# Six experts whose two batches share 448 token slots, routing scratch in PSUM, and weight loads issued at other steps

## The chip, the core and the metric

The kernel runs on one core of one Trainium2 chip. Five engines work at once, each in its own order: TensorE (PE; its weight loads are shown as PEld), VectorE (DVE), ScalarE (ACT), GpSimd (POOL) and SyncE (SP), which here only issues transfers. They wait for each other through semaphores. The metric is device time in microseconds (us) from start to end; lower is better. Of the kernel before, three runs took 550.86, 552.16 and 553.15 us, median 552.16 us.

## The reference

Three layers follow each other. The first is a gated recurrent attention (2 batches, 8 heads, 768 tokens, head size 40), which the kernel computes in chunks of 128 tokens. The second sends each of the 1536 tokens (320 wide) to its two best of 8 experts. The third is one dense layer pair with `h * cos(h)` between them.

```python
noisy_logits = x @ w_gate + np.log1p(np.exp(x @ w_noise)) * noise
top2 = np.argpartition(-noisy_logits, 2, axis=1)[:, :2]
for e in range(E):                       # 8 experts, w1[e]: 320 x 1024, w2[e]: 1024 x 320
    for k in range(2):
        mask = top2[:, k] == e
        h = np.maximum(x[mask] @ w1[e], 0.0)
        out[mask] += top2_w[mask, k, None] * (h @ w2[e])
...
h = x @ w_in                             # 1536 x 2048
g = h * np.cos(h)
return (g @ w_out).astype(np.float32)
```

## The kernel before

**Slots.** A token's row is copied into a slot of its expert, and the expert works on slots. Each expert has, for each batch, 240 slots in two tiles of 120. Experts 0 and 1 run first for batch 0 alone (groups 0 and 1, 240 slots), then experts 2 to 7 for both batches together (groups 2 to 7, four tiles, 480 slots), then experts 0 and 1 for batch 1 (groups 8 and 9). If an expert got more tokens than slots, a branch at the end would compute everything anew; the profile shows nothing of it.

**One expert step.** Each group has eight steps, one for each 128 of the 1024 hidden columns; steps are numbered 0 to 79, and `step(k)` is `expert_step(k // 8, k % 8)`. To keep float32 accuracy, every factor is split into a high part and a low part, each in a format that TensorE takes at full rate. In a step, `split` makes the high part `wh` of the weights two steps ahead on ACT and the low part `wl` on POOL (on DVE for some steps); `mm1` multiplies in eight matmuls, which stream all slots of the group; ACT takes the positive part as `hh`, DVE makes the rest `hl`; and `mm2` of the step before adds, for each tile, `hh x wh`, `hh x wl` and `hl x wh` (320 columns streamed, the tile's slots as the stationary side) into one PSUM bank per tile. After the eighth step `fin1` copies the tiles out (ACT and DVE in turn) and writes them to `YD` in DRAM.

**Routing.** For each batch, `router_a0` to `router_a3` find the two best experts and their weights, `router_b` counts with matmuls at which place of its expert a token stands, `router_b1` and `router_b2` build one-hot matrices, and `router_c` turns them with twelve matmuls into `idx`, the token of each slot. `gather` (an indirect transfer issued by POOL) then fetches the rows into `xgt`, and `prep_slot` transposes them on PE and splits them into `xh` and `xl`. Batch 0 is routed while batch 1 is still in attention; batch 1 after it, during expert steps 5 to 11. Group 2, at step 16, is the first that needs both.

**What sets the order.** Nothing is scheduled by a tool: the code's order is the order on each engine. Attention runs in twelve steps `att_step(n)`; `pre`, `mid`, `fill` and `put` hang other work at places within or behind a step `n`, and `put(k, ...)` behind expert step `k` after attention. Each engine takes its instructions strictly in this order, so an instruction that waits holds all behind it. SP's transfers are one such queue: expert weights (`load_w`, 704 KB for two of eight blocks, into one of two buffers `WB`), results to `YD`, and the third layer's weights (`conv_load`), which DVE and ACT convert during the expert steps (`conv_ops`).

**PSUM.** There are eight banks: four of tag A (`psA`), three of tag S (`psS`), and one of tag M (`psM`). What takes the one M bank (transposes, router matmuls) waits until its last user has been read out.

Of the kernel before, what the change touches and what calls it, by code (L numbers as in the profile page):

```python
# [37 lines left out]
def tile_mlstm_moe_moe2(ctx, tc, qk, kv, og, gi, gf, wcat, noise, wm1, wm2, cst, out):  # L38
# [105 lines left out]
    XD = [dr.tile([S, KW], FT, name=f"xd{b}") for b in range(B)]  # L144
# [272 lines left out]
    def router_b(b):  # L417
        r = R[b]
        p = psM()
        T.matmul(p[:, 0:NC * E + E], tri, os_.rearrange("p c e -> p (c e)"), start=True, stop=False)  # L420
# [9 lines left out]
        ge = rsm([128, 2, NC], "r_ge")  # L430
        V.tensor_scalar(ge, rr, float(SL), None, op0=OP.is_ge)
        pp = rsm([128, 2, NC], "r_pp")
        V.scalar_tensor_tensor(out=pp, in0=ge, scalar=-float(SL), in1=rr, op0=OP.mult, op1=OP.add)
        jj = rsm([128, 2, NC], "r_jj")
        V.scalar_tensor_tensor(out=jj, in0=r["ixf"], scalar=2.0, in1=ge, op0=OP.mult, op1=OP.add)
# [12 lines left out]

    def router_b2(b):
        r = R[b]  # L450
        jj = r["jj"]
# [4 lines left out]
        V.tensor_scalar(bm[:, :, :, 0, :], jm, pid, None, op0=OP.mult)
        V.tensor_tensor(out=bm[:, :, :, 1, :], in0=jm, in1=tid[:, None].to_broadcast([128, 2, NC, 16]), op=OP.mult)

    def router_c(b):
# [8 lines left out]
        hi = rsm([128, 16], "r_hi")
        V.tensor_scalar(hi[:SL], p[:SL, 16:32], 128.0, None, op0=OP.mult)
        idx = r["idx"] = cp.tile([128, 16], U32, name=f"idx{b}")  # L470
        V.tensor_tensor(out=idx[:SL], in0=p[:SL, 0:16], in1=hi[:SL], op=OP.add)


    YD = [dr.tile([NJ * SL, DM], FT, name=f"yd{b}") for b in range(B)]
# [7 lines left out]
    NSL = 4 * SL  # L482
    groups = []
    for e in (0, 1):
        groups.append((e, [(0, 2 * e), (0, 2 * e + 1)]))
    for e in range(2, E):
        groups.append((e, [(0, 2 * e), (0, 2 * e + 1), (1, 2 * e), (1, 2 * e + 1)]))
    for e in (0, 1):
# [587 lines left out]
```

## Time and profile before

| what | us |
|---|---|
| runs, median of three | 552.16 |
| the profiled execution: its own time | 549.69 |
| its span, first to last instruction | 547.1 |
| attention until expert step 5, about | 0 to 113 |
| expert steps 5 to 15 | 113.3 to 148.0 |
| expert steps 16 to 63 (groups 2 to 7) | 148.0 to 322.4 |
| expert steps 64 to 79, first combination | 322.4 to 360 |
| third layer | 360 to 547 |

All stretches are counted from the span's start. An engine that is busy all through a stretch without a gap sets that stretch's length; where it has gaps, the row says what ended each of them. TensorE's clock has two levels; the granted clock of a stretch is its mean share of the full one.

### The profile page before, as it was taken

The page shows a single profiled execution, that of the slowest core. Times are in us where ns is not written, and L with a number is a line of the kernel's source. Part 1 is how long each engine was busy: PE and PEld are TensorE (multiplying, and loading weights), DVE is VectorE, ACT ScalarE, POOL GpSimd, SP SyncE. Part 2 cuts the span into 40 slices and gives each one's busy share as a digit, 9 for nine tenths or more (in the row PEclk, how much of TensorE's full clock was granted, in tenths as well). Part 3 has the DMA queues.
Part 4 walks back from the last instruction along what each step waited for, and adds up shares of the span by engine and source line. Part 5 has one row for each costly group of instructions (what it writes and reads, how often), then busy time and mean ns, then how long its engine had stood idle before and what let it go on. Part 6 is the DMA issues. An engine that isn't in the chain of part 4 may idle for free.

```text
span 547.1 us, 9061 instructions
## 1 busy us (share of the span) xinstructions
PE 506.9 (93%) x3244; PEld 480.0 (88%) x3244; DVE 381.8 (70%) x733; ACT 326.3 (60%) x689; POOL 277.9 (51%) x247
## 2 busy tenths in 40 slices
PE   3899879987699999999999998899999999999994
PEld 2788768987599999999999997799999999999994
DVE  8874585578338687767677458969967756777772
ACT  3567863454345554445445455657878878777772
POOL 6435556647374756576666568746535633300000
PEclk9999998898899999999999999999999999999999
DMA  6888980366383755647283719341101101001001
GB/s 177 245 278 277 315 298 29 97 226 240 101 281 113 234 183 186 232 146 270 92 326 103 287 33 359 118 124 37 37 1 62 48 1 37 2 1 37 0 1 43
DMA packets 25668, 77.67 MB, mean 142 GB/s; under 512 B 3888, under 2 KB 11152, under 8 KB 25616
## 3 DMA queue, kind: packets, MB, share of 16 engines
q1 hardware_dynamic: 22416, 67.18, 36.0%
q0 software_dynamic: 3200, 9.84, 6.2%
q8 instruction: 27, 0.44, 0.3%
q14 instruction: 25, 0.20, 0.1%
HBM read 67.72 MB, written 9.29 MB: 141 GB/s over the span
## 4 chain that ended last, share of the span: by engine, by line
PE 71%; DMA 11%; DVE 8%; POOL 3%; ACT 3%; issue 3%; SPq 0%; POOLq 0%; ACTq 0%; DVEq 0%
PE pS L543 33%; PE pA L552 11%; PE pA L549 11%; PE pA L548 10%; DMA xgt<-xd,idx 4%; DMA qk<-qk 3%; PE pM L505 2%; POOL wl L536 2%; DMA gb<-gd 2%; PE pS L307 1%; ACT wt L206 1%; DMA gd<-g_all 1%; PE pA L244 1%; PE pM L348 1%; DMA raw<-wm 1%
## 5 line engine op out<-in xcount | busy, mean ns | idle before, releaser
L536 POOL TENSOR_TENSOR wl<-wraw,wh 128x704 fp32r<-128x704 f32 x70 | 122.6, 1756 | 84.0 <-ACT wh L534 79.6
L582 DVE SCALAR_TENSOR_TENSOR hl<-pS,hh 128x480 fp32r<-128x480 f32 (+1 forms) x80 | 44.3, 555 | 55.6 <-ACT hh L581 54.9
L534 ACT ACTIVATE wh<-wraw 128x704 fp32r<-128x704 f32 x80 | 63.0, 787 | 23.6 <-PE pA L552 19.8
L549 PE MATMUL pA<-wl,hh 128*120 128x320 f32 x256 | 77.0, 312 | 0.0
L548 PE MATMUL pA<-wh,hh 128*120 128x320 f32 x256 | 76.9, 311 | 0.0
L695 POOL TENSOR_TENSOR hl<-m_t,hh 128x384 fp32r<-128x384 f32 x41 | 41.8, 1020 | 61.4 <-ACT hh L693 40.6
L543 PE MATMUL pS<-xh,wh 128*128 128x480 f32 (+1 forms) x240 | 72.4, 356 | 0.0
L543 PE MATMUL pS<-xh,wl 128*128 128x480 f32 (+1 forms) x240 | 69.1, 342 | 0.3 <-POOL wl L536 0.3
L543 PE MATMUL pS<-xh,w 128*128 128x384 f32 x288 | 66.8, 341 | 0.8 <-DVE m_t L689 0.8
L581 ACT ACTIVATE hh<-pS 128x480 fp32r<-128x480 f32 (+1 forms) x80 | 39.0, 488 | 30.7 <-PE pS L543 30.2
L552 PE MATMUL pA<-wh,hl 128*120 128x320 f32 x256 | 51.7, 314 | 6.0 <-DVE hl L582 6.0
L675 ACT ACTIVATE m_t<-pS,magic 128x384 f32<-128x384 f32 x64 | 37.2, 581 | 28.7 <-PE pS L543 27.6
L543 PEld LDWEIGHTS pS<-xh,w 128*128 128x128 f32 x288 | 49.7, 188 | 1.9 <-DVE m_t L689 1.9
L549 PEld LDWEIGHTS pA<-wl,hh 128*120 128x120 f32 x256 | 47.0, 184 | 1.8
L548 PEld LDWEIGHTS pA<-wh,hh 128*120 128x120 f32 x256 | 47.1, 184 | 1.4
L543 PEld LDWEIGHTS pS<-xh,wl 128*128 128x128 f32 x240 | 43.8, 193 | 4.9 <-POOL wl L536 0.5
L552 PEld LDWEIGHTS pA<-wh,hl 128*120 128x120 f32 x256 | 40.4, 183 | 7.8 <-DVE hl L582 7.8
L507 ACT ACTIVATE xh<-pM 128x360 fp32r<-128x360 f32 (+1 forms) x42 | 20.0, 477 | 45.1 <-PE pM L505 44.9
L689 DVE SCALAR_TENSOR_TENSOR m_t<-m_t,pS 128x384 f32<-128x384 f32 x64 | 35.3, 552 | 12.4 <-ACT m_t L688 12.2
L549 PE MATMUL pA<-w,hh 128*128 128x320 f32 x144 | 42.9, 309 | 0.0
L548 PE MATMUL pA<-w,hh 128*128 128x320 f32 x144 | 42.9, 308 | 0.0
L543 PEld LDWEIGHTS pS<-xh,wh 128*128 128x128 f32 x240 | 41.4, 193 | 1.5
(160 smaller groups left out, 1195.3 us busy)
## 6 DMA issues: line engine op xcount, KB each, us to landing
wraw<-wm SPq DMA_DIRECT2D x36, 704.0 KB
raw<-wm SPq DMA_DIRECT2D x16, 704.0 KB
qk<-qk SPq DMA_DIRECT2D x24, 240.0 KB
gb<-gd SPq DMA_DIRECT2D x10, 512.0 KB
yd<-yt SPq DMA_DIRECT2D x26, 150.0 KB
kv<-kv SPq DMA_DIRECT2D x12, 324.0 KB
wraw<-wm SPq DMA_DIRECT2D x8, 352.0 KB
xd<-xt SPq DMA_DIRECT2D x12, 192.0 KB
```

What stands on the lines that cost most here:

```text
L507: A.activation(xh[:, :, sl], pv, AF.Copy)
L534: A.activation(wh, raw[:, f, :], AF.Copy)
L536: eng.tensor_tensor(out=wl, in0=raw[:, f, :], in1=wh.bitcast(FT), op=OP.subtract)
L543: T.matmul(p[:, :n], w[:, 128 * k:128 * k + 128], x[:, m, :], start=(i == 0), stop=(i == 7))
L548: T.matmul(a[:np_, :DM], hh[:, s], wh[:, KW:], start=first, stop=False)
L549: T.matmul(a[:np_, :DM], hh[:, s], wl[:, KW:], start=False, stop=False)
L552: T.matmul(a[:np_, :DM], hl[:, s], wh[:, KW:], start=False, stop=last)
L581: A.activation(hh[:, :n], p[:, :n], AF.Relu)
L582: V.scalar_tensor_tensor(out=hl[:, :n], in0=p[:, :n], scalar=0.0, in1=hh[:, :n].bitcast(FT), op0=OP.max, op1=OP.subtract)
L675: A.activation(t, m["p"], AF.Identity, bias=magic, scale=0.5 / PI)
L689: V.scalar_tensor_tensor(out=s, in0=s, scalar=1.0, in1=m["p"], op0=OP.subtract, op1=OP.mult)
L695: eng.tensor_tensor(out=m["hl"], in0=m["t"], in1=m["hh"].bitcast(FT), op=OP.subtract)
```

## The change

- Groups 2 to 7 have 448 slots for the tokens of both batches together, in tiles of 128, 128, 128 and 64. The batch 1 ranks of experts 2 to 7 start from batch 0's counts (`router_s`, one more matmul in `router_b`). Groups 0, 1, 8 and 9 keep 240, in tiles of 128 and 112.
- `hh` and `hl` lie in one tile `hb` of 896 columns, so that the 64 `hh` columns and the 64 `hl` columns of the fourth tile are neighbours. `mm2h` loads them as one stationary side of 128 columns and multiplies by `wh` and `wl`: two matmuls where there were three. DVE makes `hl` in two instructions (384 and 64 columns), and `fin1` adds the two halves.
- Much of the router's scratch lies in the M bank (`r["q"]`). For batch 1, `pp`, `jj` and `jm` do too; for batch 0 `r_jj`, `r_pp` and `r_jm` stay in SBUF. One-hot matrices are 128 and 32 wide (before 120 and 16).
- Batch 1's routing calls stand earlier, `prep_slot(1, ...)` uses `psA`, and the low part of step 7's weights is made on POOL.
- Expert 1's weights load behind attention steps 9 to 11 and step 5, expert 2's behind steps 6 to 8 (before 9 to 15). Three transfers behind attention step 8 fill the unused rows of `YD`, which is now one tensor, as is `XD`.

```diff
+    def mm2h(a, wh, wl, hb, first, last):
+        T.matmul(a[:, :DM], hb[:, 384:512], wh[:, KW:], start=first, stop=False)
+        T.matmul(a[:, :DM], hb[:, 384:512], wl[:, KW:], start=False, stop=last)
...
-        V.scalar_tensor_tensor(out=hl[:, :n], in0=p[:, :n], scalar=0.0, in1=hh[:, :n].bitcast(FT),
-                               op0=OP.max, op1=OP.subtract)
+        for a, z, o in ((0, min(n, 384), 512), (384, n, 448)):
+            if a < n:
+                V.scalar_tensor_tensor(out=hb[:, o:o + z - a], in0=p[:, a:z], scalar=0.0,
+                                       in1=hh[:, a:z].bitcast(FT), op0=OP.max, op1=OP.subtract)
...
+            if i == 3:
+                A.activation(t[:64, :DM], a[64:128, :DM], AF.Copy)
+                V.tensor_tensor(out=t[:64, :DM], in0=a[:64, :DM], in1=t[:64, :DM], op=OP.add)
...
-    POOL_SPLIT = (1, 9, 11, 65, 67, 75)
+    POOL_SPLIT = (1, 7, 9, 11, 65, 67, 75)
...
-    for i in range(3):
-        put((6, 7, 6)[i], load_w, 1, 2 + 2 * i, 2)
-    put(5, router_a0, 1)
-    put(5, router_a1, 1)
-    put(5, prep_slot, 1, 0)
-    put(6, prep_slot, 1, 1)
+    put(5, load_w, 1, 6, 2)
     put(5, router_a2, 1)
-    put(7, router_a3, 1)
-    put(7, router_b, 1)
-    put(8, router_b1, 1, 0)
-    put(9, router_b1, 1, 1)
-    put(9, router_b2, 1)
-    put(11, router_c, 1)
+    put(5, prep_slot, 1, 0, psA)
+    put(6, prep_slot, 1, 1, psA)
+    put(6, router_b, 1)
+    put(7, router_b1, 1, 0)
+    put(7, router_b1, 1, 1)
+    put(8, router_b2, 1)
+    put(9, router_p, 1)
+    put(9, router_c, 1)
+    put(10, router_a3, 1)
     for i in range(4):
-        put(11 + i // 2, gather, 2, i)
-        put(13 + i // 2, prep_slot, 2, i)
+        put(10 + i // 2, gather, 2, i)
+        put(12 + i // 2, prep_slot, 2, i)
...
-            put(9 + 8 * i + 2 * h, load_w, e, 2 * h, 2)
+            put(9 + 8 * i + 2 * h if i else (6, 6, 7, 8)[h], load_w, e, 2 * h, 2)
```

`router_a0(1)` and `router_a1(1)` are called before step 5, right behind attention's last matmuls.

**The second matmul pair on PE.** These are PE's rows for the `mm2` of one step of groups 2 to 7 (`pA` is the tile's bank), before:

```order
L548 MATMUL pA<-wh,hh 120x320 [waits Activation_49]
L549 MATMUL pA<-wl,hh 120x320
...
L552 MATMUL pA<-wh,hl 120x320 [waits DVE_49]
L552 MATMUL pA<-wh,hl 120x320 x3
L543 MATMUL pS<-xh,wh 128x480 [waits Activation_49]
```

and now:

```order
L587 MATMUL pA<-wh,hb 128x320 [waits Activation_49]
L588 MATMUL pA<-wl,hb 128x320
...
L591 MATMUL pA<-wh,hb 128x320 [waits DVE_49]
L591 MATMUL pA<-wh,hb 128x320 x2
L599 MATMUL pA<-wh,hb 128x320 [waits DVE_49]
L600 MATMUL pA<-wl,hb 128x320
L582 MATMUL pS<-xh,wh 128x448 [waits Activation_49]
```

The `hh` pair stood four times and stands three times; the fourth tile's pair comes last, behind the three `hl` matmuls.

**Batch 1's routing on DVE**, from the count to the one-hot matrices, before (`hl` and `yt` belong to the expert steps):

```order
L425 TENSOR_TENSOR r_rk<-pM,r_oh_1358 128x96 [waits PE_49]
L427 TENSOR_REDUCE flag<-pM 128x1
L429 TENSOR_REDUCE r_rr<-r_rk 128x12 [waits DVE_49]
L431 TENSOR_SCALAR r_ge<-r_rr 128x12 [waits DVE_49]
L433 SCALAR_TENSOR_TENSOR r_pp<-r_ge,r_rr 128x12 [waits DVE_49]
L435 SCALAR_TENSOR_TENSOR r_jj<-r_ixf,r_ge 128x12
L436 TENSOR_SCALAR r_rr<-r_rr 128x12 [waits DVE_49]
L438 SCALAR_TENSOR_TENSOR r_pos_1443<-r_ixf,r_rr 128x12 [waits DVE_49]
L582 SCALAR_TENSOR_TENSOR hl<-pS,hh 128x240 [waits Activation_49]
L560 COPY yt<-pA 120x320 [waits PE_49]
L446 TENSOR_TENSOR r_am<-cc,r_pp 128x720
```

and now:

```order
L440 TENSOR_TENSOR pM<-pM,r_oh_1356 128x96 [waits DVE_49,PE_49]
L443 TENSOR_REDUCE pM<-pM 128x12 [waits DVE_49]
L444 TENSOR_SCALAR pM<-pM 128x12 [waits DVE_49]
L448 TENSOR_SCALAR r_jj<-pM 128x12 [waits DVE_49]
L449 SCALAR_TENSOR_TENSOR pM<-r_jj,pM 128x12 [waits DVE_49]
L451 TENSOR_SCALAR pM<-pM 128x12 [waits DVE_49]
L637 SCALAR_TENSOR_TENSOR hb<-pS,hb 128x240 [waits Activation_49]
L476 TENSOR_TENSOR r_am<-pM,cc 128x768 [waits DVE_49]
```

The place of a token (`L438`) and the overflow flag are now made later, and every row up to `r_am` has at least one side in the M bank.

**Weight loads on SP** around the end of attention, before:

```order
L480 DMA wraw<-wm 128x1408 [waits DMAHW3_49]
L563 DMA yd_111<-yt 120x320 [waits DMAHW4_49,Activation_49]
L563 DMA yd_111<-yt 120x320 [waits DMAHW5_49,DVE_49]
L480 DMA wraw<-wm 128x1408 [waits DMAHW6_49,Pool_49]
```

and now:

```order
L521 DMA wraw<-wm 128x1408 [waits DMAHW6_49]
L521 DMA wraw<-wm 128x1408 [waits DMAHW0_49,DMAHW7_49,DVE_49,Pool_49]
L521 DMA wraw<-wm 128x1408
L521 DMA wraw<-wm 128x1408 [waits DMAHW1_49]
L616 DMA yd<-yt 128x320 [waits DMAHW2_49,Activation_49]
```

The first load of expert 2 (the row that waits for POOL) stood behind the two writes of group 0's results and stands ahead of them, with two more loads.

## Rows read from the trace of the kernel before

**Rows 1.** The page's first part: busy time of TensorE, share of the span, instructions, and the same of its weight loads and the other engines.

```profile
PE 506.9 (93%) x3244; PEld 480.0 (88%) x3244; DVE 381.8 (70%) x733; ACT 326.3 (60%) x689; POOL 277.9 (51%) x247
```

**Rows 2.** Busy time by stretch: from and to, length, then busy us and instructions of PE, PEld, DVE, ACT and POOL, the granted clock, the share of the DMA engines and GB/s.

```profile
73.80:88.00 14.20, 11.86 (x70) 10.71 (x69) 13.69 (x29) 6.93 (x17) 9.99 (x12) 0.76 0.52 173
...
113.30:148.00 34.70, 26.32 (x194) 24.88 (x193) 22.96 (x70) 15.61 (x34) 17.86 (x13) 0.90 0.59 211
148.00:322.40 174.40, 174.40 (x1023) 162.35 (x1022) 120.74 (x152) 84.90 (x142) 111.20 (x71) 1.00 0.56 193
322.40:360.00 37.60, 33.00 (x247) 30.94 (x247) 30.30 (x48) 21.92 (x43) 31.17 (x23) 1.00 0.55 194
```

**Rows 3.** PE in order of time, from the end of step 22's `mm1` to the start of step 24: start, us from the first's start to the last's end, what, and how many.

```profile
170.71 0.38 PE L543 MATMUL pS<-xh,wl 128*128 128x480 f32 x1
...
172.69 0.47 PE L505 MATMUL pM<-ident,xgt 120*128 120x120 f32 x3
172.92 0.68 PE L543 MATMUL pS<-xh,wh 128*128 128x480 f32 x2
...
174.52 0.38 PE L543 MATMUL pS<-xh,wl 128*128 128x480 f32 x1
174.74 0.31 PE L548 MATMUL pA<-wh,hh 128*120 128x320 f32 x1
...
175.91 0.75 PE L552 MATMUL pA<-wh,hl 128*120 128x320 f32 x4
176.49 0.60 PE L543 MATMUL pS<-xh,wh 128*128 128x480 f32 x2
```

**Rows 4.** The same in the third layer, where a stationary side has 128 columns.

```profile
410.05 0.31 PE L548 MATMUL pA<-w2q,hh 128*128 128x320 f32 x1
410.20 0.31 PE L549 MATMUL pA<-w2q,hh 128*128 128x320 f32 x1
...
410.93 0.60 PE L552 MATMUL pA<-w2q,hl 128*128 128x320 f32 x3
411.37 0.86 PE L543 MATMUL pS<-xh,w 128*128 128x384 f32 x4
```

**Rows 5.** Groups of instructions by line and shape: count, busy us, mean ns of one, idle time before them and what ended it.

```profile
L549 PEld LDWEIGHTS pA<-wl,hh 128*120 128x120 f32 x256 | 47.0, 184 | 1.8
...
L677 DVE SCALAR_TENSOR_TENSOR m_t<-pS,m_t 128x384 f32<-128x384 f32 x64 | 35.7, 558 | 2.2
...
L582 DVE SCALAR_TENSOR_TENSOR hl<-pS,hh 128x480 fp32r<-128x480 f32 x48 | 31.5, 657 | 45.1 <-ACT hh L581 44.6
...
L549 PEld LDWEIGHTS pA<-w,hh 128*128 128x128 f32 x144 | 27.0, 188 | 0.0
...
L582 DVE SCALAR_TENSOR_TENSOR hl<-pS,hh 128x240 fp32r<-128x240 f32 x32 | 12.8, 403 | 10.6 <-ACT hh L581 10.3
```

**Rows 6.** DVE in order of time, during batch 0's routing, batch 1's routing and step 22.

```profile
75.89 1.66 DVE L435 SCALAR_TENSOR_TENSOR r_jj<-r_ixf,r_ge 128x12 f32<-128x12 f32 x1
...
77.66 1.12 DVE L438 SCALAR_TENSOR_TENSOR r_pos<-r_ixf,r_rr 128x12 uint32<-128x12 f32 x1
...
123.23 1.37 DVE L431 TENSOR_SCALAR r_ge<-r_rr 128x12 f32<-128x12 f32 x1
124.63 1.59 DVE L433 SCALAR_TENSOR_TENSOR r_pp<-r_ge,r_rr 128x12 f32<-128x12 f32 x1
126.14 0.16 DVE L435 SCALAR_TENSOR_TENSOR r_jj<-r_ixf,r_ge 128x12 f32<-128x12 f32 x1
...
127.26 0.90 DVE L446 TENSOR_TENSOR r_am<-cc,r_pp 128x720 bf16<-128x720 f32 x1
...
131.10 0.32 DVE L456 TENSOR_SCALAR r_bm<-r_jm,cc 128x192 bf16<-128x192 f32 x1
...
173.84 0.66 DVE L582 SCALAR_TENSOR_TENSOR hl<-pS,hh 128x480 fp32r<-128x480 f32 x1
```

**Rows 7.** POOL in order of time, at the same two routings.

```profile
75.84 1.68 POOL L536 TENSOR_TENSOR wl<-wraw,wh 128x704 fp32r<-128x704 f32 x1 [0.76 <-ACT wh L534]
...
122.87 3.32 POOL L536 TENSOR_TENSOR wl<-wraw,wh 128x704 fp32r<-128x704 f32 x2 [1.03 <-ACT wh L534]
...
131.03 1.00 POOL L497 DMA_INDIRECT xgt<-xd,idx  x1 [0.18 <-issue]
```

**Rows 8.** PE in order of time: batch 1's twelve index matmuls, and its gaps (in brackets the idle time before the row and what ended it).

```profile
81.05 1.22 PE L244 MATMUL pA<-qk 128*128 128x256 f32 x2 [2.20 <-DVE ppt L253]
...
127.00 0.55 PE L552 MATMUL pA<-wh,hl 128*120 128x320 f32 x2 [2.81 <-DVE hl L582]
...
132.52 0.78 PE L465 MATMUL pM<-r_bm,r_am 128*120 128x32 bf16 x12
...
140.74 0.50 PE L505 MATMUL pM<-ident,xgt 120*128 120x120 f32 x3 [2.76 <-DMA xgt<-xd,idx]
...
145.92 0.50 PE L505 MATMUL pM<-ident,xgt 120*128 120x120 f32 x3 [1.35 <-ACT xh L507]
```

**Rows 9.** The chain that ended last, two pieces: start, us, what.

```profile
94.07 3.13 DMA xgt<-xd,idx
...
132.34 8.27 DMA xgt<-xd,idx
```

**Rows 10.** SP's transfers in order of time.

```profile
127.81 1.92 SPq L480 DMA_DIRECT2D wraw<-wm  x4
```

More of the change, by code (lines that the diff above doesn't have):

```diff
@@ L26 @@
 F2 = 2048
-SL = 120
-CAP = 2 * SL
-NJ = 2 * E
+CAP1 = 240
+CAP2 = 448
+NJ = 32
+ROWS = NJ * C
+ROW0 = [0, 256] + [512 * e - 512 for e in range(2, E)]
+ROW1 = [3584, 3840] + ROW0[2:]
 KW = 384
@@ L143, in tile_mlstm_moe_moe2 @@
         STS.append(t)
-    XD = [dr.tile([S, KW], FT, name=f"xd{b}") for b in range(B)]
+    XD = dr.tile([B * S, KW], FT, name="xd")
     KO = H * D
@@ L428, in router_b @@
-        rr = rsm([128, 2, NC], "r_rr")
+        rr, y = (q[:, 440 + 12 * i:452 + 12 * i].rearrange("p (k c) -> p k c", c=NC) for i in range(2))
         V.tensor_reduce(rr, rk, axis=AX.X, op=OP.add)
[L430 to L435, printed above, removed]
@@ L436, in router_b @@
-        V.tensor_scalar(rr, rr, float(CAP - 1), None, op0=OP.min)
-        pos = r["pos"] = rsm([128, 2, NC], f"r_pos{b}", U32)
-        V.scalar_tensor_tensor(out=pos, in0=r["ixf"], scalar=float(CAP), in1=rr, op0=OP.mult, op1=OP.add)
-        r["pp"], r["jj"] = pp, jj
+        V.tensor_scalar(y, rr, -63.75, MAGIC7, op0=OP.add, op1=OP.add)
+        js = rsm([128, 2, NC], "r_jj")
+        jj, pp = ((q[:, 464 + 12 * i:476 + 12 * i].rearrange("p (k c) -> p k c", c=NC) for i in range(2)) if b else
+                  (js, rsm([128, 2, NC], "r_pp")))
@@ L441, in router_b1, with router_s @@
+    def router_s():
+        so = rsm([128, E], "r_so")
+        V.tensor_reduce(so, os_[:, 0:NC].rearrange("p c e -> p e c"), axis=AX.X, op=OP.add)
+        V.tensor_tensor(out=so, in0=so, in1=joint, op=OP.mult)
+        V.tensor_tensor(out=rb[:, 1], in0=so, in1=row1, op=OP.add)
     def router_b1(b, k):
@@ L464, in router_c @@
             for c in range(NC):
-                T.matmul(p[:SL, 0:32], r["am"][:, k, c, :], r["bm"][:, k, c].rearrange("p a j -> p (a j)"),
+                T.matmul(p[:, 0:2 * NJ], r["am"][:, k, c, :], r["bm"][:, k, c].rearrange("p a j -> p (a j)"),
                          start=(n == 0), stop=(n == 2 * NC - 1))
                 n += 1
[L468 to L474, printed above, removed]
+        hi = rsm([128, NJ], "r_hi")
+        if b == 0:
+            V.tensor_scalar(hi, p[:, NJ:2 * NJ], 128.0, None, op0=OP.mult)
+            V.tensor_tensor(out=idx0, in0=p[:, 0:NJ], in1=hi, op=OP.add)
+            V.tensor_scalar(idxe, idx0[:, 0:4], float(S - 1), None, op0=OP.min)
+        else:
+            V.scalar_tensor_tensor(out=hi, in0=p[:, NJ:2 * NJ], scalar=128.0, in1=idx0, op0=OP.mult, op1=OP.add)
+            V.tensor_tensor(out=hi, in0=p[:, 0:NJ], in1=hi, op=OP.add)
+            V.tensor_scalar(idx, hi, float(B * S - 1), None, op0=OP.min)
+    idx0 = cp.tile([128, NJ], FT, name="idx0")
+    idxe = cp.tile([128, 4], U32, name="idxe")
+    idx = cp.tile([128, NJ], U32, name="idx")
+    YD = dr.tile([ROWS, DM], FT, name="yd")
     WB = {}
@@ L480, in load_w @@
         Y.dma_start(WB[e][:, i:i + n, :], wm1[e, :, i:i + n, :])
[L482 to L488, printed above, removed]
-        groups.append((e, [(1, 2 * e), (1, 2 * e + 1)]))
+    T2, T4 = (128, 112), (128, 128, 128, 64)
+    groups = [(e, T2, 2 * e) for e in (0, 1)]
+    groups += [(e, T4, 4 * e - 4) for e in range(2, E)]
+    groups += [(e, T2, 28 + 2 * e) for e in (0, 1)]
     NG = len(groups)
@@ L853, in tile_mlstm_moe_moe2 @@
     mid[9] = [(router_b1, (0, 1))]
+    put(8, router_s)
     fill[9] = [(router_c, (0,)), (gather, (0, 0)), (gather, (0, 1))]
```

197 lines of the change are left out of this document (121 added, 76 removed).

## The prediction

> **What bounds the kernel now.** I read the shares first, then the stretches, then PE's own order, then the gaps and what ended them. PE is busy 506.9 of 547.1 us [rows 1], so only PE's work or PE's gaps can move the time. By stretch the two are apart [rows 2]: in steps 16 to 63 PE is busy 174.40 of 174.40 us at full clock, so that stretch is as long as its matmuls. In steps 5 to 15 it is busy 26.3 of 34.7 us at a mean clock of 0.90, so 8.4 us are gaps, and up to 3.4 us (a tenth of the stretch) go to the lower level, 1.2 instead of 2.4 GHz. The gaps have names [rows 8]: 2.81 us for `hl` from DVE, 2.76 us for gathered rows, 1.35 us for the one M bank between two transposes. DVE was late because `L431` and `L433`, with everything in SBUF and only 12 columns, took 1.37 and 1.59 us where their neighbour took 0.16 [rows 6]; they ended as POOL's two splits did, 3.32 us from 122.87 on [rows 7]. `hl`, which reads PSUM, kept its 403 ns there [rows 5]. The gathered rows were late because four weight transfers had been issued in one burst at 127.81 [rows 10], just ahead of the gather at 131.03 [rows 7]: the next one took 8.27 us to land, where one at 94.07 took 3.13 [rows 9].
>
> **Groups 2 to 7.** Start to start, a matmul of 480 columns takes 0.22 us (174.52 to 174.74) and one of 320 takes 0.147 (1.17 us for eight from 174.74 to 175.91) [rows 3]. That is 0.46 ns a column. 32 columns less on eight matmuls are 8 x 0.0146 = 0.117 us a step, and one matmul of 320 less is 0.147 us. 0.264 us x 48 steps = 12.7 us.
>
> Stationary sides grow from 120 to 128 columns. The third layer has 128, and its matmuls also follow at 0.15 and, over three, 0.44 us [rows 4], so I cost this at nothing: the load (188 ns, before 184 [rows 5]) lies beside the matmul before it. The transposes move nearly as many columns as before, 0.23 us a tile [rows 3]: nothing.
>
> What hides DVE's and ACT's part is the distance from the end of `mm1` to the first `hl` matmul. In step 22 that is 171.09 (170.71 + 0.38) to 175.91 [rows 3], and `hl` ended at 174.50 [rows 6]: 1.41 us to spare. Now the distance loses 0.147 + 0.117 + two `hh` matmuls 0.293 = 0.56 us. `hl` in two instructions costs 558 ns for 384 columns [rows 5], and about 216 ns for 64 by the line through 403 (240 columns) and 657 (480 columns) [rows 5]: 774, so 0.12 us more. About 0.7 us is left. DVE's load rises from 120.7 of 174.4 us [rows 2] to 126.3 of 161.7, 78%. I take no loss, with an upper bound of 4 us: a stall of 0.7 us in about six steps with two weight conversions. The third copy of `fin1` on ACT, and the addition that follows on DVE, come ahead of nine matmuls and an `mm1`, some 2.9 us, before the fourth bank is written again: nothing.
>
> **Steps 5 to 15.** I lay the new order out from 113.3 with the durations of the rows. PE's own work is 26.3 us busy less 3.4 for the clock = 22.9 us; by pieces it is 11 steps x (8 x 0.11 + 6 x 0.147) = 19.4, six transposes of 0.23, and router matmuls of about 1.0 with the twelve that took 0.78 [rows 3, 8], 21.8. I take 22.9. The gaps that I expect:
> - Batch 1's top-two work begins one step earlier on ACT and DVE, and PE reaches the count matmuls at about 117.2; four small DVE rows of 0.2 us end at 117.9. Gap 0.7.
> - The six rows behind the count have a PSUM side, so I cost them at 0.2 us each, not at the 1.4 and 1.6 of rows 6. Then come two `r_am` of 0.95 (0.90 for 720 columns [rows 6], now 768), one `hl`, one copy and three one-hot rows of 0.5 (0.32 for 192 columns [rows 6], now 384): 125.4. PE reaches the twelve matmuls at 123.9. Gap 1.5.
> - `idx` stands at 126.9. POOL's queue has seven splits in a row now (step 7's is new), 1.66 us each [rows 7], and is free at 126.6. Gathers go out at 127.0 and each 1.3 us later, and land 3.1 us later [rows 9]: 130.1 to 134.0. Expert 2's first three transfers left at about 117, when POOL had done step 7's split, so the burst is over. PE asks for the first at 131.6: no gap.
> - Twice, two tiles are prepared back to back through the M bank: 1.3 us each time [rows 8], 2.6.
> - About 0.6 us for `hl` rows that stand behind router rows.
>
> Sum 5.4; the stretch takes 22.9 + 5.4 = 28.3 us, and no gap is as long as the 2.2 us and more after which the clock fell (0.76 in the stretch with the 2.20 us gap [rows 2, 8]). Gain 6.4 us. Bounds: no gap goes away but the clock's loss is the same (gain 0), or all go (22.9, gain 11.8). I take the value between because each gap is worked out from its own rows.
>
> **Before step 5.** Batch 0's `r_jj` and `r_pos` waited for POOL, 1.66 and 1.12 us [rows 6], the first until POOL's split from 75.84 on ended [rows 7], and PE then stood 2.20 us for `ppt` [rows 8]. Those two now read PSUM and are free of it, minus 2.4 us. But `r_jm` and `r_bm` of batch 0 are still wholly in SBUF and twice as wide: `r_jm` comes early enough to meet the same split, `r_bm` POOL's next work. By the rows' pattern I get `ppt` about 0.5 us later than before; bounds -2.4 and +2. `router_s` adds three rows that nothing waits for at once. One DVE row more before the first gather costs 0.2 us, and an expert 1 load that now runs beside the second gather 0.3 (bounds 0 and 1.5). Sum: +1.0 us.
>
> **Tail and third layer.** In steps 64 to 79 [rows 2] the shapes stay 240 columns and the DVE order is the same; the third layer only names its buffers otherwise. Nothing, bounds -1 and +1.5.
>
> **Sum.** -12.7 - 6.4 + 1.0 = -18.1 us. The profiled execution's own time is 549.69, which gives 531.6. The median of the runs is 2.47 us above it, so I predict 534.1 us.
>
> A rule weighed: a stationary load of 128 columns took 188 ns against 184 for 120, in rows that follow at the same 0.147 us [rows 3 to 5]. The Trainium skill (page "TensorE: Matmul & The Clock Gate", section "LDWEIGHTS (loading the stationary operand)") states a load's time as its columns divided by 1.2 ns, so wider tiles cost more; by its figures an estimate of 6.7 ns a load on 11 loads in 48 steps is 3.5 us, which would make 537.6. The trace agrees that a load grows with its columns, but shows it beside a matmul.
>
> **Rivals.**
> 1. The wait only moves. For: POOL's seven splits in a row, 11.7 us, run at about PE's pace, and the one M bank holds router scratch longer. Then steps 5 to 15 keep their 34.7 us: 552.2 - 12.7 + 1.0 = 540.5. Against: two of the old gaps have a cause that goes. Chance 0.17.
> 2. PE's clock stays up in batch 0's routing: `ppt` comes 2.4 us earlier, the 2.20 us gap goes, and so does the lower level behind it, 0.24 x 14.2 = 3.4 us [rows 2]. 534.1 - 1.5 - 2.2 - 3.4 = 527.0. Against: the two wider SBUF rows. Chance 0.10.
> 3. Weight loads stand in the open: 4 ns [rows 5] x 11 x 48 = 2.1 us, 536.2. Against it: rows 4. Chance 0.03.
> 4. Slower: DVE becomes the bound in groups 2 to 7. `hl` now has two instructions behind the conversions on a DVE at 78%, ACT's `hh` waits behind a conversion that waits for DVE, and PE has 0.7 us to spare. At 2 us a conversion, 12 conversions cost 24 us: 558. It decides from a latency (end of `mm1` to end of `hl`) of 4.26 us; before, step 22 had 3.41. Slower than now needs 18.1 / 12 = 1.5 us beyond that. Chance 0.06.
> 5. The change doesn't do what it says: more than 448 tokens for one of experts 2 to 7, and the branch computes all anew, over 100 us more. The mean is 3072 / 8 = 384. Chance 0.01.
>
> **How the numbers follow.** The forecast has 0.63, with its own range of 530 to 539 (the bounds of each stretch seldom fall on one side together). With rivals 1 to 3 the range becomes 526 to 542, which leaves out about 0.15. About 0.5% of the time, 2.8 us, is what a measurement of this kernel can tell from no change. The forecast and rivals 1 to 3 are all faster by more, 0.93. Of rivals 4 and 5, 0.05 are slower and 0.02 end near zero.
>
> **What would show it.** Steps 17 to 63 take about 3.24 us (3.50 now) without PE gaps. The router rows of batch 1 in the M bank take about 0.2 us beside POOL's splits. Gathers of group 2 land in 3 to 4 us, and step 16 starts about 5.4 us earlier, near 142.6. PE's gap before the attention step that follows batch 0's count is still 2 to 3 us, and the clock falls behind it. A gap before the `hl` matmuls in groups 2 to 7, or a step 16 later than 147, would make the prediction wrong.

## The result, and the profile after

Four runs of the changed kernel took 534.16 to 537.66 us, median 535.19; four of the kernel before, on the same chip, 550.86 to 554.38, median 552.65. The ratio is 0.969 (95% interval 0.964 to 0.974). The forecast was 534.1 us, 526 to 542. The four times go with the granted clock of the execution: 534.16 and 534.54 us at 0.987 and 0.988, 535.85 (the profiled one) at 0.982, 537.66 at 0.979. Run once more beside the last experiments (`e12_after`), it took 532.28 against 552.61: 0.964 (0.959 to 0.969). The profiled executions, cut at the first matmul of a step:

| stretch, us | before | after | after, once more | forecast change |
|---|---|---|---|---|
| to step 5 | 113.3 | 114.6 | 113.5 | +1.0 |
| steps 5 to 15 | 34.7 | 30.6 | 28.1 | -6.4 |
| steps 16 to 63 | 174.3 | 162.6 | 162.8 | -12.7 |
| steps 64 to 79 | 37.5 | 38.4 | 38.5 | 0 |
| third layer | 187.2 | 187.9 | 187.9 | 0 |
| span | 547.1 | 534.1 | 530.6 | -18.1 |

Busy time and share of the span (as [rows 1]), and stretches of the first profile after, as in [rows 2]. The first two are attention's, where PE's clock (the column behind POOL's) fell, the third is steps 5 to 15, the fourth a part of it:

```profile
PE 496.5 (93%) x3198; PEld 474.1 (89%) x3198; DVE 374.3 (70%) x789; ACT 326.9 (61%) x695; POOL 282.7 (53%) x248
```

```profile
60.00:75.00 15.00, 12.33 (x76) 10.69 (x75) 6.67 (x36) 7.96 (x24) 6.42 (x10) 0.77 0.95 301
80.00:92.00 12.00, 9.60 (x57) 8.12 (x56) 11.54 (x21) 5.64 (x18) 8.78 (x10) 0.86 0.39 104
114.60:145.21 30.61, 24.91 (x195) 23.57 (x194) 18.65 (x72) 15.89 (x34) 18.98 (x14) 0.94 0.53 191
133.00:141.00 8.00, 4.48 (x23) 3.99 (x21) 3.30 (x8) 2.52 (x5) 2.00 (x2) 0.79 0.08 29
145.20:307.90 162.70, 162.58 (x976) 155.68 (x975) 116.14 (x198) 84.84 (x147) 113.68 (x71) 1.00 0.56 203
```

Groups 2 to 7 are as full as before, PE busy 162.58 of 162.70 us at full clock, and shorter. PE in order, from the end of step 21 to step 25, answers to [rows 3]:

```profile
164.30 0.31 PE L600 MATMUL pA<-wl,hb 128*128 128x320 f32 x1
164.45 0.49 PE L544 MATMUL pM<-ident,xgt 128*128 128x128 f32 x3
164.70 0.66 PE L582 MATMUL pS<-xh,wh 128*128 128x448 f32 x2
...
167.86 0.31 PE L600 MATMUL pA<-wl,hb 128*128 128x320 f32 x1
168.10 0.40 PE L544 MATMUL pM<-ident,xgt 64*128 64x64 f32 x3
168.42 0.47 PE L582 MATMUL pS<-xh,wh 128*128 128x448 f32 x1
...
171.75 0.57 PE L582 MATMUL pS<-xh,wh 128*128 128x448 f32 x2
...
174.98 0.36 PE L582 MATMUL pS<-xh,wh 128*128 128x448 f32 x1
```

Step 24, a pure step (no transposes between its matmuls), takes 3.23 us (171.75 to 174.98), before 3.51. Step 22 takes 3.72, before 3.84: only 0.12 less. The tile of 64 rows, the smallest, takes longest: 0.56 us from the matmul ahead of it to the one behind (167.86 to 168.42), where 128 rows take 0.40 (164.30 to 164.70).

DVE, batch 1's routing, as in [rows 6]; every row has a side in PSUM (`pM`), and POOL's splits ran beside them:

```profile
121.56 0.17 DVE L448 TENSOR_SCALAR r_jj<-pM 128x12 f32<-128x12 f32 x1
121.77 0.17 DVE L449 SCALAR_TENSOR_TENSOR pM<-r_jj,pM 128x12 f32<-128x12 f32 x1
...
124.82 0.56 DVE L485 TENSOR_TENSOR pM<-pM,cc 128x384 f32<-128x384 f32 x1
125.41 0.62 DVE L487 TENSOR_SCALAR r_bm<-pM,cc 128x384 bf16<-128x384 f32 x1
```

The same two one-hot rows for batch 0, in SBUF, took more than twice as long:

```profile
79.41 1.46 DVE L485 TENSOR_TENSOR r_jm<-r_jj,cc 128x384 f32<-128x384 f32 x1
80.91 1.31 DVE L487 TENSOR_SCALAR r_bm<-r_jm,cc 128x384 bf16<-128x384 f32 x1
```

PE's gaps, as in [rows 8]: in attention, before the index matmuls, and between group 2's preparations:

```profile
64.75 1.19 PE L247 MATMUL pA<-qk 128*128 128x256 f32 x2 [2.05 <-DMA qk<-qk]
...
84.06 0.70 PE L247 MATMUL pA<-qk 128*128 128x256 f32 x2 [1.87 <-DVE ppt L256]
...
127.01 0.52 PE L497 MATMUL pM<-r_bm,r_am 128*128 128x64 bf16 x12 [1.90 <-DVE r_fl L461]
...
132.78 0.49 PE L544 MATMUL pM<-ident,xgt 128*128 128x128 f32 x3
135.66 0.52 PE L544 MATMUL pM<-ident,xgt 128*128 128x128 f32 x3 [2.39 <-DVE xh L548]
...
141.26 0.37 PE L544 MATMUL pM<-ident,xgt 64*128 64x64 f32 x3 [1.39 <-ACT xh L546]
```

The waits for `hl` (2.81 us) and for gathered rows (2.76) are gone. Left are the index matmuls, released by the flag's row `r_fl`, and the M bank, twice. After the gap of 2.39 the clock fell (0.79 over 133 to 141 us), and the `mm2` matmuls behind it followed at 0.27 us instead of 0.147. PE's busy time tells the same: 24.91 us here, 23.35 in `e12_after`, where the clock stayed up in these steps.

### The profile page after: what moved, and what is told of

Same layout as the page of the kernel before. It is cut to its first block, busy times and chain, and to the rows that moved or that the text cites. A ratio compares the mean times of both kernels' runs of the same rounds, so it can differ in the third digit from the quotient of the medians.

```text
span 534.1 us, 9038 instructions
## 1 busy us (share of the span) xinstructions
PE 496.5 (93%) x3198; PEld 474.1 (89%) x3198; DVE 374.3 (70%) x789; ACT 326.9 (61%) x695; POOL 282.7 (53%) x248
## 4 chain that ended last, share of the span: by engine, by line
PE 72%; DVE 12%; DMA 7%; issue 3%; ACT 2%; POOL 2%; SPq 1%; POOLq 0%; DVEq 0%; ACTq 0%
PE pS L582 33%; PE pA L591 10%; PE pA L588 10%; PE pA L587 10%; DMA qk<-qk 4%; PE pM L544 2%; DMA gb<-gd 2%; PE pS L310 1%; PE pA L600 1%; PE pA L599 1%; PE pA L247 1%; PE pM L351 1%; DVE hb L637 1%; DVE xt L667 1%; DVE c_t L706 1%
## 5 line engine op out<-in xcount | busy, mean ns | idle before, releaser
L637 DVE SCALAR_TENSOR_TENSOR hb<-pS,hb 128x384 fp32r<-128x384 f32 (+2 forms) x128 | 46.0, 390 | 50.8 <-ACT hb L634 47.4
L582 PE MATMUL pS<-xh,wh 128*128 128x448 f32 (+1 forms) x240 | 69.8, 345 | 0.0
L582 PE MATMUL pS<-xh,wl 128*128 128x448 f32 (+1 forms) x240 | 66.7, 332 | 0.9 <-POOL wl L575 0.9
L587 PE MATMUL pA<-wh,hb 128*128 128x320 f32 x208 | 62.6, 310 | 0.0
L588 PE MATMUL pA<-wl,hb 128*128 128x320 f32 x208 | 62.6, 310 | 0.0
L634 ACT ACTIVATE hb<-pS 128x448 fp32r<-128x448 f32 (+1 forms) x80 | 37.7, 471 | 28.6 <-PE pS L582 19.5
L591 PE MATMUL pA<-wh,hb 128*128 128x320 f32 x208 | 44.5, 314 | 3.8 <-DVE hb L637 3.8
L753 POOL TENSOR_TENSOR wl<-m_t,wh 128x384 fp32r<-128x384 f32 x25 | 25.4, 1016 | 37.6 <-ACT wh L751 23.3
L582 PE MATMUL pS<-xl,wh 128*128 128x448 f32 (+1 forms) x160 | 39.8, 331 | 0.0
L587 PEld LDWEIGHTS pA<-wh,hb 128*128 128x128 f32 x208 | 38.9, 187 | 0.7
L588 PEld LDWEIGHTS pA<-wl,hb 128*128 128x128 f32 x208 | 38.9, 187 | 0.5
L591 PEld LDWEIGHTS pA<-wh,hb 128*128 128x128 f32 x208 | 33.3, 187 | 5.6 <-DVE hb L637 5.5
```

The lines of the kernel that those rows point to most:

```text
L582: T.matmul(p[:, :n], w[:, 128 * k:128 * k + 128], x[:, m, :], start=(i == 0), stop=(i == 7))
L587: T.matmul(a[:n, :DM], hh[:, s], wh[:, KW:], start=first, stop=False)
L588: T.matmul(a[:n, :DM], hh[:, s], wl[:, KW:], start=False, stop=False)
L591: T.matmul(a[:n, :DM], hl[:, s], wh[:, KW:], start=False, stop=last)
L634: A.activation(hh[:, :n], p[:, :n], AF.Relu)
L637: V.scalar_tensor_tensor(out=hb[:, o:o + z - a], in0=p[:, a:z], scalar=0.0, in1=hh[:, a:z].bitcast(FT), op0=OP.max, op1=OP.subtract)
```

## The experiments

Each starts from the changed kernel. "Steps 5 to 15" and the like are read from one profile, ratios from timed runs against the kernel before.

**The fourth tile with three matmuls** (and `fin1` without its addition):

```diff
-        T.matmul(a[:, :DM], hb[:, 384:512], wh[:, KW:], start=first, stop=False)
-        T.matmul(a[:, :DM], hb[:, 384:512], wl[:, KW:], start=False, stop=last)
+        T.matmul(a[:64, :DM], hb[:, 384:448], wh[:, KW:], start=first, stop=False)
+        T.matmul(a[:64, :DM], hb[:, 384:448], wl[:, KW:], start=False, stop=False)
+        T.matmul(a[:64, :DM], hb[:, 448:512], wh[:, KW:], start=False, stop=last)
...
```

> The changed kernel with one part undone: the fourth tile of groups 2 to 7 takes three matmuls again (hh by wh, hh by wl, hl by wh, each 64 slots stationary), and its result needs no addition of two halves. Theory (PE's matmuls alone set groups 2 to 7): one matmul of 320 columns more is 0.147 us in each of 48 steps, so a pure step goes from 3.23 to 3.38 us, steps 16 to 63 from 162.7 to 169.7, and the ratio to the kernel before from 0.969 to 0.982. Rival A (DVE, ACT or the feeding of weights already set part of these steps): less than 4 us. Rival B (a stationary side of 64 columns costs more or less than one of 128, per matmul): a step of 3.30 or 3.45 us.

The theory came. A pure step took 3.37 us (+0.14), steps 16 to 63 169.0 (+6.4 where 7.0 were expected; 0.3 of the rest is a wait in step 28, 3.87 us in the changed kernel and 3.70 here), ratio 0.984 (0.977 to 0.990). PE's matmuls set these steps, and a matmul of 320 columns cost the same with 64 stationary columns as with 128.

**480 columns in `mm1`**, on top of `e5_pad64` below (the fourth tile is prepared 96 columns wide for it):

```diff
...
-        mm1(p, n, wh, wl, d["xh"], d["xl"])
+        mm1(p, 480 if n == 448 else n, wh, wl, d["xh"], d["xl"])
```

> The kernel with the padded fourth tile (e5_pad64), where mm1 of groups 2 to 7 streams 480 columns instead of 448; the last 32 are not used. Theory (0.46 ns a column, as the forecast has it): 8 matmuls x 32 columns x 0.46 ns = 0.117 us, so a pure step takes 3.35 us where it took 3.23, and steps 16 to 63 take 5.6 us more than in e5_pad64. Rival (the load of the stationary side sets the distance of these matmuls in part): a step of 3.23 to 3.29 us.

A pure step took 3.35 us, and steps 16 to 63 took 167.66 against 162.04 us: +5.6. That this is the expected sum to the tenth is luck: `e5_pad64` has a wait in step 28 (4.18 us, here 3.69) that this run hasn't. Step for step the difference is 0.13 us where 0.117 were expected, in 48 steps 6.2, or 0.51 ns a column against the forecast's 0.46. The columns set the distance, and the price was a tenth too low. Ratio 0.981 (0.972 to 0.990).

**The fourth tile with 128 rows** in gather and transposes:

```diff
-        n = sz[i]
+        n = 128 if i == 3 else sz[i]
...
```

> The changed kernel, where the fourth tile of groups 2 to 7 is gathered and transposed with 128 rows (64 more than it has slots; only the first 64 columns are used). In the changed kernel a tile of 64 rows takes PE 0.565 us from the last matmul before its transposes to the matmul behind them, a tile of 128 rows 0.393. Theory (a transposed tile with 64 of 128 rows holds PE up, and this is the 0.8 us by which steps 16 to 63 miss the forecast): steps 22, 30, 38, 46 and 54 go from 3.73 to 3.55 us, steps 16 to 63 from 162.7 to 161.9, ratio 0.968. Rival (64 more gathered rows, and ACT's and DVE's part, set these steps): they stay at 3.73 us.

```profile
167.62 0.31 PE L602 MATMUL pA<-wl,hb 128*128 128x320 f32 x1
167.77 0.49 PE L545 MATMUL pM<-ident,xgt 128*128 128x128 f32 x3
168.01 0.65 PE L584 MATMUL pS<-xh,wh 128*128 128x448 f32 x2
```

The tile now takes 0.39 us (167.62 to 168.01), the step 3.56. Steps 16 to 63 took 162.0, not 161.9, since step 28 waited longer ahead of its transposes in that execution (4.18 against 3.87 us); for this place the profiles of `e10_best`, `e11_best_spread` and `e12_after` name a gathered row. Ratio 0.971 (0.963 to 0.979), too wide to show 0.8 us; the rows show it. The edit changes the rows and the columns of these transposes together, so which of the two counts is not shown.

**Batch 1's scratch in SBUF again** (the diff shows `jj`, `pp` and `jm`; the rank products, ranks and rounded ranks went back too):

```diff
...
-        jj, pp = ((q[:, 464 + 12 * i:476 + 12 * i].rearrange("p (k c) -> p k c", c=NC) for i in range(2)) if b else
-                  (js, rsm([128, 2, NC], "r_pp")))
+        jj, pp = (rsm([128, 2, NC], "r_jj1") if b else js, rsm([128, 2, NC], "r_pp"))
...
-        jm = (r["q"][:, 0:384].rearrange("p (k c j) -> p k c j", k=2, j=NJ) if b else
-              rsm([128, 2, NC, NJ], "r_jm"))
+        jm = rsm([128, 2, NC, NJ], "r_jm")
```

> The changed kernel with batch 1's scratch behind the count (rank products, ranks, rounded ranks, jj, pp and the one-hot jm) in SBUF again; the order is the changed one. Theory (rows with all sides in SBUF wait for POOL's weight splits): at least two of the 12-column rows between the count and r_am take 1.2 to 1.7 us instead of 0.17, jm or one r_bm row takes over 1.2 us, and PE's gap before the twelve index matmuls grows from 1.9 to 4 to 6 us; steps 5 to 15 take 33 to 36 us, with the clock's lower level once more. Rival (the earlier place of these rows was what counted; POOL's splits are met by chance): the rows take 0.2 us, the gap stays at 1.9 and steps 5 to 15 within 0.7 us of 30.6.

```profile
123.26 0.17 DVE L449 TENSOR_SCALAR r_jj<-r_y 128x12 f32<-128x12 f32 x1
123.47 1.68 DVE L450 SCALAR_TENSOR_TENSOR r_pp<-r_jj,r_rr 128x12 f32<-128x12 f32 x1
...
127.92 1.42 DVE L485 TENSOR_TENSOR r_jm<-r_jj,cc 128x384 f32<-128x384 f32 x1
129.38 1.71 DVE L487 TENSOR_SCALAR r_bm<-r_jm,cc 128x384 bf16<-128x384 f32 x1
```

```profile
123.45 1.68 POOL L575 TENSOR_TENSOR wl<-wraw,wh 128x704 fp32r<-128x704 f32 x1 [0.25 <-ACT wh L573]
127.24 1.68 POOL L575 TENSOR_TENSOR wl<-wraw,wh 128x704 fp32r<-128x704 f32 x1 [2.12 <-ACT wh L573]
129.16 1.71 POOL L575 TENSOR_TENSOR wl<-wraw,wh 128x704 fp32r<-128x704 f32 x1 [0.24 <-ACT wh L573]
```

Steps 5 to 15 took 34.3 us, as the theory has it, at the clock's lower level from 130.4 to 137.2; `hl` came 1.63 us late and PE's gap before the index matmuls was 3.87. Of the 12-column rows only one, where two were expected, took over 1.2 us; two of the wide rows did. Each slow row lasts until a split of POOL ends, or a little longer. The scratch in PSUM is worth 3.7 us against the first profile, and more against the second; ratio 0.979 (0.971 to 0.986). By the Trainium skill (page "SBUF — State Buffer", section "Who interferes with whom") a DVE instruction with two SBUF inputs contends with a GpSimd instruction that reads SBUF, and one with at most one SBUF input, outside certain modes, doesn't. These rows agree: 1.68 us with two SBUF inputs, 0.17 in the changed kernel with one. `L487`, whose only tile is in SBUF beside a column of constants, took 1.71 us too; whether it ran in one of those modes no run shows.

**Expert 2's loads at 9, 11, 13 and 15**:

```diff
-            put(9 + 8 * i + 2 * h if i else (6, 6, 7, 8)[h], load_w, e, 2 * h, 2)
+            put(9 + 8 * i + 2 * h, load_w, e, 2 * h, 2)
```

> The changed kernel with expert 2's four weight loads behind steps 9, 11, 13 and 15 again, as in the kernel before. Theory (a gather issued beside a burst of weight transfers lands late, and this is what the move of the loads took away): the gathers of group 2 land 5 to 8 us after their issue where the changed kernel shows about 4, PE waits for gathered rows again, and steps 5 to 15 take 32 to 35 us where they took 30.6. Rival A (the old wait came from POOL's late issue and the M bank; the loads are of no account): steps 5 to 15 stay within 0.7 us of 30.6. Rival B (the weights of expert 2 themselves come too late for the splits two steps ahead): a gap at steps 14 to 18 for wh, and no longer landing of the gathers.

```profile
136.09 0.52 PE L544 MATMUL pM<-ident,xgt 128*128 128x128 f32 x3 [1.99 <-DMA xgt<-xd,idx]
```

The loads left in one burst again, the first gather, issued at 129.64, was awaited until 136.0, and steps 5 to 15 took 31.6 us (ratio 0.981, 0.977 to 0.985). The mechanism is there. By this profile its size is 1.0 us more than 30.6, where 1.4 to 4.4 were expected; but the profiled execution took 538.19 us at a granted clock of 0.984, the other three 540.05 to 542.23 at 0.970 to 0.978. By the timed runs the place of the loads is worth more: the interval lies wholly above the changed kernel's 0.964 to 0.974, 6 to 7 us by the middle values (each against the kernel before on its own chip). Where the rest is lost the profile doesn't show.

**Group 2's tiles through two banks**:

```diff
-        put(12 + i // 2, prep_slot, 2, i)
+        put(12 + i // 2, prep_slot, 2, i, psM if i % 2 else psA)
```

> The changed kernel, where the first and third tile of group 2 are transposed through a bank of tag A and only the second and fourth through the M bank, so that no two preparations in a row share a bank. Theory (the one M bank makes the 2.39 us and 1.39 us gaps between two preparations, and the first of them drops the clock, 1.7 us more over 3.4 us): both gaps go, the clock stays up, and steps 5 to 15 take 25.5 to 27 us instead of 30.6; ratio 0.960 to 0.963. Rival (the gathered rows land too late anyway: about 133, 135 and 136): PE waits for the gathers at the second and third tile instead, 1.5 to 3 us in all, and steps 5 to 15 take 28 to 30 us.

```profile
133.74 0.49 PE L544 MATMUL pA<-ident,xgt 128*128 128x128 f32 x3
134.18 0.52 PE L544 MATMUL pM<-ident,xgt 128*128 128x128 f32 x3
...
136.32 0.49 PE L544 MATMUL pA<-ident,xgt 128*128 128x128 f32 x3
137.29 0.37 PE L544 MATMUL pM<-ident,xgt 64*128 64x64 f32 x3 [0.49 <-ACT hb L634]
```

Both gaps went, the clock stayed up there, and the stretch took 25.7 us: the theory's number. The gathered rows were not in the way. The ratio, 0.965 (0.960 to 0.970), is above the expected 0.960 to 0.963: in this profile step 5 started at 115.6 us, 1.0 later than in the changed kernel's first, and steps 64 to 79 took 0.5 longer.

**Batch 1's routing at its old steps**, scratch and loads as changed:

```diff
-    put(6, router_b, 1)
+    put(7, router_b, 1)
...
-    put(9, router_c, 1)
+    put(11, router_c, 1)
...
-        put(12 + i // 2, prep_slot, 2, i)
+        put(13 + i // 2, prep_slot, 2, i)
...
```

> The changed kernel with batch 1's routing calls at the steps of the kernel before (top-two work behind step 5, count behind 7, one-hot rows behind 8 and 9, index matmuls behind 11, gathers behind 11 and 12, preparation behind 13 and 14) and step 7's low weights on DVE; the scratch in the M bank and the earlier weight loads stay. Theory (the earlier place is worth something by itself: every wait of this chain now ends two steps before group 2 needs it): steps 5 to 15 take 33 to 35 us where they took 30.6, with PE waiting for gathered rows again. Rival (scratch and loads bring the whole gain, and the place only moves the same gaps): steps 5 to 15 stay within 0.7 us of 30.6.

Steps 5 to 15 took 28.0 us. Neither number came, but beside the 28.1 of `e12_after` the rival's sense did: the place is worth nothing that one profile can show, nor do the timed runs on the same chip show anything (532.18 against 532.28 us).

**Two edits in attention**: batch 0's one-hot rows behind step 8, and expert 0's loads spread.

```diff
-    mid[8] = [(router_b2, (0,))]
+    put(8, router_b2, 0)
```

> The changed kernel, where batch 0's one-hot rows (r_jm and two r_bm, all in SBUF) stand behind attention step 8 on DVE instead of ahead of its ppt. In the changed kernel they took 1.46, 1.31 and 0.54 us there, PE then waited 1.87 us for ppt at 84.06, and its clock fell for 3.4 us. Theory (these SBUF rows, held by POOL, are what the forecast's +1.0 us before step 5 stands for): the gap falls below 0.5 us, the clock stays at full level between 80 and 90 us, and step 5 starts 2.5 to 3.5 us earlier, at 111 to 113. Rival (DVE has the same work one step later, with the ppt of that step behind it): the gap moves behind it, to about 92 to 96 us, and step 5 starts within 1 us of 114.6 to 115.8.

```diff
-        put((4, 4, 4, 6, 6, 7, 7, 9)[i], load_w, 0, i, 1)
+        put((5, 6, 6, 7, 7, 8, 8, 9)[i], load_w, 0, i, 1)
```

> The changed kernel with expert 0's eight weight loads behind attention steps 5, 6, 6, 7, 7, 8, 8, 9 in place of 4, 4, 4, 6, 6, 7, 7, 9. In the changed kernel PE waits 2.05 us for the keys and queries of attention step 9 at 64.75 us, which were issued behind three weight loads at 52.6, and then runs at the lower level for 6.8 us; the kernel before waited 1.62 us there and stayed at full clock. Theory (the weight burst makes the keys late, and the gap drops the clock): the gap shrinks below 1 us, the clock stays at full level from 60 to 75 us, and step 5 starts 3 to 5 us earlier, at 110 to 112. Rival (attention's own transfers fill the queues; the later loads only collide with the next step's): the gap stays or moves to 72 to 76 us, and step 5 starts within 1 us of 114.6 to 115.8.

The first took the `ppt` gap away, and step 5 started at 113.3, between the two numbers; but a gap of 1.39 us came at 91.1, and the clock was low for half of the time from 80 to 101 us (0.76 granted). Since the unchanged order later started step 5 at 113.5 as well, this shows no gain. The second took the 2.05 us gap away, and the clock stayed up there; a gap of 1.10 us came at 70.8, the `ppt` gap stayed at 1.87 with a longer low stretch behind it, and step 5 started at 114.5. Both rivals were right in kind: attention's gaps move. Ratios 0.973 (0.965 to 0.982) and 0.974 (0.966 to 0.981).

**Composed**, and the changed kernel again:

```diff
-        put(12 + i // 2, prep_slot, 2, i)
+        put(12 + i // 2, prep_slot, 2, i, (psA, psM, psS, psM)[i])
...
-    put(9, router_p, 1)
     put(9, router_c, 1)
+    put(10, router_p, 1)
...
-        p = psM()
+        p = (psA if b else psM)()
...
```

> The changed kernel with four edits: group 2's tiles transposed through banks of tags A, M, S, M in turn; batch 1's index matmuls into a bank of tag A, with token places and the flag behind them; the fourth tile gathered and transposed with 128 rows; batch 0's one-hot rows behind attention step 8. Theory (the gains add up, since they lie in three stretches): steps 5 to 15 take 25 to 26 us, steps 16 to 63 162 us, step 5 starts 1 to 2 us earlier than without the last edit; ratio 0.955 to 0.960. Rival (the clock's lower level falls on other stretches as gaps move, and takes the gain back): ratio 0.963 to 0.968.

> As e10_best, and expert 0's weight loads behind attention steps 5, 6, 6, 7, 7, 8, 8, 9. Theory (with batch 0's one-hot rows out of ppt's way, the gap at 64 us that this takes away no longer comes back behind it): step 5 starts at 110 to 112 us and the ratio is 0.950 to 0.957. Rival (attention's gaps keep moving, as in e6_spread): step 5 starts at 113 to 115 us, and the ratio is that of e10_best.

> The changed kernel once more, beside the two composed ones. Theory (its time is settled): ratio 0.964 to 0.974; steps 5 to 15 take 30 to 31 us, a low stretch of the clock near 64 to 72 us of 3.4 or 6.8 us. Rival (the 30.6 us of the first profile were one execution's luck): steps 5 to 15 below 29 or above 32 us.

`e10_best` took 530.01 us (0.959, 0.956 to 0.963), steps 5 to 15 25.4 and steps 16 to 63 162.0 us, as its theory has them; step 5 at 113.6 is no earlier than the changed kernel's 113.5 on that chip, so the fourth edit shows no gain. `e11_best_spread` took 526.58 (0.953, 0.949 to 0.957). Its interval lies wholly below that of the changed kernel on the same chip (0.959 to 0.969), so it beats both kernels. The theory on the spread loads stays open: its ratio came, its start of step 5 (110 to 112 us) did not, with 113.8. But that profile is of an execution of 529.74 us at a granted clock of 0.977, with lower levels at 69.9 to 76.8, 90.4 to 100.7 and 322.5 to 325.9 us; the other four took 526.15 to 526.60 at 0.988 to 0.991, and of these no profile tells where step 5 starts.

For `e12_after` the rival's sign came: steps 5 to 15 took 28.1 us, below 29, so the 30.6 is no settled time; and the clock was low at 81.0 to 87.8 us, not near 64 to 72. In steps 5 to 15 it stayed at full level, and the M bank's gap was 1.39 where the first profile had 2.39:

```profile
131.66 0.49 PE L544 MATMUL pM<-ident,xgt 128*128 128x128 f32 x3
133.54 0.52 PE L544 MATMUL pM<-ident,xgt 128*128 128x128 f32 x3 [1.39 <-DVE xh L548]
```

## Why the prediction was right

**Groups 2 to 7, forecast -12.7, measured -11.7.** Both prices held: a pure step lost 0.27 us (forecast 0.264); undone, the columns gave 5.6 us back (6.2 step for step) where 5.6 were priced, the third matmul 6.4 of 7.1. What hides DVE's part held too: the two `hl` instructions took 556 and 214 ns (forecast 558 and 216), and no `hl` gap showed:

```profile
L637 DVE SCALAR_TENSOR_TENSOR hb<-pS,hb 128x384 fp32r<-128x384 f32 x48 | 26.7, 556 | 39.5 <-ACT hb L634 39.0
L637 DVE SCALAR_TENSOR_TENSOR hb<-pS,hb 128x64 fp32r<-128x64 f32 x48 | 10.3, 214 | 0.0
```

DVE was busy 71% of the time, not 78. The step that failed is "the transposes move nearly as many columns as before": the tile of 64 rows costs 0.17 us more than one of 128, and five such steps are 0.8 us of the 1.0. Another 0.3 is the wait in step 28.

**Steps 5 to 15, forecast -6.4 (28.3 us), measured -4.1 (30.6), and 28.1 the second time.** The scratch in PSUM, the loads and the M bank were the right causes, each shown by its own run; the earlier place of the calls, which the forecast laid out as well, was worth nothing that a run shows. The gaps came out at 5.7 us in sum where 5.4 were forecast, but not as forecast: those of 0.7 at the count and 0.6 for `hl` didn't come, and the others were longer by 1.6. What the sum missed is PE's own time, 24.9 us where 22.9 were taken: at full clock it is 23.35, and 1.6 more went to the lower level. The second profile met 28.3 by two errors that cancel:

```profile
113.47:141.52 28.05, 23.35 (x196) 22.04 (x194) 18.66 (x72) 15.81 (x34) 18.98 (x14) 1.00 0.58 209
```

Mis-sized were, then, two gaps, the clock, and by 0.4 us PE's own work. The gap before the index matmuls was 1.90, not 1.5: they take the M bank, which the place and flag rows still read, behind one `hl`; with another bank, and these rows behind, it was 1.43 in `e10_best`. The first M-bank gap was 2.39, not 1.3. And "no gap is as long as the 2.2 us and more after which the clock fell" failed: it fell after the 2.39 us gap, and in two other runs (`e5_pad64`, `e6_spread`) after the one before the index matmuls, 1.89 us there. Of the seven profiled executions with this order unchanged, six took 29.6 to 30.6 us, and only the last met the forecast. In four of the seven ACT's `xh` starts 0.9 to 1.0 us after the first tile's transposes (133.27 to 134.30 in the first profile), in the others at once. The chain shows these transposes held on PE until then (132.94 to 134.28); what holds them no row names, and that is open.

**Before step 5, forecast +1.0, measured +1.3 and +0.1.** Batch 0's small rows got free of POOL and the wider SBUF ones met it, as forecast; the `ppt` gap was 1.87 us, and the clock fell behind it. Not foreseen was the gap for keys and queries, 2.05 us at 64.75, after which the clock was low for 6.8 us. In `e6_spread` and `e11_best_spread`, with the weight loads spread, it is gone, which speaks for the burst as its cause. In the nine profiles that leave attention as changed, step 5 starts anywhere from 113.5 to 115.8 us, +0.1 to +2.4, so that +1.0 fits is no evidence for its parts, which no run tried one by one.

**Tail, forecast 0, measured +0.9 and +0.7 us** (steps 64 to 79 and the third layer): PE waited 1.70 us for one `hl` at 327.47, where the kernel before waited 0.97 us (at 341.14). It stood behind weight conversions of 1.81 and 2.70 us on DVE, before 1.30 and 2.47. `e9_order`, `e10_best` and `e12_after` have the same wait at 1.74 or 1.75 us. Why the conversions take longer no run tried.

**The sum.** The spans differ by 13.0 and 16.5 us, the medians by 17.5 and 20.3; the forecast had 18.1. That the median came within 1.1 us of 534.1 is in part luck: by the first pair of profiles the terms missed by 5.1 us, all to one side, by the second by 1.6. The kernel before took 549.69 us in its profiled execution and 552.65 in the median, the changed one 535.85 and 535.19, and this difference made up for the miss. Of the rivals, the first (the wait only moves) holds in part: a third of the forecast gain in steps 5 to 15 stayed behind as the M bank's wait and the clock. The second, that the clock stays up behind batch 0's routing, did not come in these profiles (`ppt` gaps of 1.87 and 1.88 us, the clock low behind them); the 1.5 us in its sum stands on no row. DVE did not become the bound, and no load stood in the open.

## What to carry to other kernels

Where PE is full and its clock is up, price a change by the start-to-start distance of its matmuls; that came out within 0.7 us on terms of 5.6 and 7.1 us. Do the same for transposes of an odd shape, which column counts alone put at nothing here. Where PE has gaps, moving a cause is worth less than its gap: ask what ends last once it is gone (here one shared PSUM bank), give that a second buffer in the same edit, and count the clock behind each gap that stays. Put small VectorE scratch in PSUM when GpSimd streams SBUF beside it.

## What was not expected of the hardware

- The transposes of a tile of 64 rows held PE longer than those of one of 128 (0.56 against 0.40 us), in all five steps that have them.
- Gaps of like length had different ends: behind the `ppt` gap of 1.87 or 1.88 us the clock was low for 3.4 us in the first profile of the changed kernel and for 6.8 in the second (0.86 and 0.72 granted over 80 to 92 us). Behind the gap of 1.90 us before the index matmuls it stayed up in both, and behind 1.89 us there it fell in `e5_pad64` and `e6_spread`.

```profile
80.00:92.00 12.00, 10.19 (x62) 9.07 (x62) 9.40 (x22) 5.17 (x16) 7.51 (x9) 0.72 0.32 81
```
